# A ConvNeXt-V2 block on one core: convolution in two stretches, larger gelu tiles, statistics in halves

## The chip, the cores and the metric

The kernel runs on one core of one Trainium2 chip. The metric is device time in microseconds (us), the median of several runs; less is better. The engines are TensorE (PE in the profile, PEld for its weight loads), VectorE (DVE), ScalarE (ACT), GpSimd (POOL) and SyncE (SP, which here only issues DMAs).

## The reference

```python
# x: 1 x 512 x 512 x 96, dw: 3 x 3 x 96, w1: 96 x 384, w2: 384 x 96, all bf16
for i in range(3):
    for j in range(3):
        out = out + xp[:, i:i+H, j:j+W, :] * dw[i, j]      # depthwise 3 x 3, zero padding
h = _layernorm(out, axis=-1)                               # over the 96 channels
h = gelu(einsum('bhwc,ce->bhwe', h, w1))                   # tanh form
gx = sqrt((h * h).sum(axis=(1, 2), keepdims=True) + 1e-6)  # over all pixels
nx = gx / (gx.mean(axis=-1, keepdims=True) + 1e-6)
h = grn_gamma * (h * nx) + grn_beta + h
return x + einsum('bhwe,ec->bhwc', h, w2)
```

The sum of squares over all pixels stands between the two matrix products, so the kernel has a first part (convolution, layernorm, first product, gelu, sums of squares) and a second part (second product and the output), for which gelu values are kept, stored or computed again.

## The kernel before, in words

The image is cut into 128 blocks of GR = 4 rows, 2048 pixels by 96 channels each. The first part is a software pipeline of slots `s = 0, 1, 2, ...`. In one slot each engine works on different blocks: block `s` is convolved, the statistics of block `s - 2` are summed, another block is normalised on POOL, and the block that was convolved 14 slots or so earlier gets its first product and gelu. A dictionary `at[(s, kind)]` tells which block has which stage in which slot. Every engine object is wrapped in `InOrder`, so each engine's instructions stand in exactly the order in which the Python code calls them, and the profile shows line 35 (the wrapper) for nearly all of them; one goes by tiles.

The steps around the change, by engine:

- **Convolution, PE.** `conv_taps` makes 72 matmuls per block, in 9 rounds of 8. A matmul has 64 input rows (h = 0 or 1: upper or lower half of the array) and 32 output columns (j = 0 to 3), so the 8 of a round lie beside each other in the array. They add into three PSUM banks, `Y3` (banks 4 to 6), one for each third `i` of the channels. Both halves h write to the same bank, at different times: a bank that one half has just left may not be entered by the other half until the first half's matmuls have ended. Before, the rounds were grouped into three bursts `conv(0)`, `conv(1)`, `conv(2)` of 24 matmuls; in a burst half 0 works on bank `n` and half 1 on bank `n + 1`. Between bursts PE is drained (`pe.drain()`), except behind `conv(1)` in slots with a gelu stage, where other work stands between.
- **Evacuation, ACT.** `evac` copies `Y3` to the tile `y_bf` as bf16 (one ACTIVATE of 3 banks). The next block's convolution can't begin before that, since there is only one `Y3`.
- **Product and gelu, PE and ACT.** `mlp_units` gives `unit(bank, n)`: matmuls that fill `n` of a block's 12 banks of results and one gelu ACTIVATE over them into the tile `g`. It uses PSUM banks 0 to 3: before, a unit of two took banks 0 and 1 together, a unit of one bank 2 or 3 in turn.
- **Statistics, PE and DVE.** `stage_stats` sums `y_bf` and its square `ysq` (made by POOL) over channels with 12 + 12 tiny matmuls into a region S of PSUM bank 7. After each batch of 4 blocks `stage_moments` on DVE reads S (tile `mom`) and clears it.
- **Sums of squares.** `squares` are `bn_stats` on DVE over `g` (tile `bst`); for what they don't cover, `gram_next` gives 6 PE matmuls of `g` with itself (a region of bank 7).
- **Input.** `turn_x` on DVE transposes the loaded block (`xin` to `xT`).
- **The rest.** POOL squares `y_bf` (`ysq`) and normalises (`yn`); SP writes `yn` to DRAM and reads it back in the layout of the product (`ynT`).

114 blocks (0 to 113) pass through the slot with convolution and gelu that the change edits; the last 14 go through `mlp_tail`, without a convolution beside it. The order of calls in such a slot was: conv(0), units 0 (2 banks) and 2 (1), conv(1), units 3 (1) and 4 (2), gram_next, units 6 (1) and 7 (1), conv(2), evacuation, gram_next, units 8 (2), 10 (1), 11 (1), with the statistics between the last two.

Of the kernel before, what the change touches and what calls it, by code (L numbers as in the profile page):

```python
# [12 lines left out]
GR = 4  # L13
# [6 lines left out]
WHOLE = (0, 3, 7)  # L20
NTAIL = 14
GRB = 3


class InOrder:
# [31 lines left out]
def kernel(  # L57
# [20 lines left out]
    NI = C // 32  # L78
# [103 lines left out]
    PS = pspool.tile([128, 8, W], f32, name="PS")  # L182
    p2 = ExitStack()
    SL = PXP + 2
    with ExitStack() as p1:
# [214 lines left out]
        n = 0  # L400
# [55 lines left out]
        ybf, ysq, yns, rbcs, msts, rns, rts = ({} for _ in range(7))  # L456
# [5 lines left out]
        def conv_taps(b, spare):  # L462
            if spare:
                Ua, Ub = banks(2), banks(1)
                Y = [Ua[:, 0, :], Ua[:, 1, :], Ub[:, 0, :]]
            else:
                Y = [Y3[:, i, :] for i in range(NI)]
            mms = []
            for n in range(3):
                mms.append([(h, j, (n + h) % NI, dx) for dx in (0, -1, 1) for j in range(GR) for h in range(2)])  # L470
            flat = [m for ms in mms for m in ms]
            first = {}
            last = {}
            for n, (h, j, i, dx) in enumerate(flat):
                first.setdefault((i, j), n)
                last[i, j] = n

            def burst(n, fence=True):
                k = sum(len(ms) for ms in mms[:n])
                for h, j, i, dx in mms[n]:  # L480
                    src = b + shift(h, j)
                    o0, o1 = max(0, -dx), W - max(0, dx)
                    pe.matmul(
                        Y[i][32 * j:32 * j + 32, o0:o1],
                        lhsT=Wq[64 * h:64 * h + 64, i, dx + 1, j, :],
                        rhs=x_rows(src, 64 * h, 64 * h + 64, i, MB * (1 + dx) + o0, o1 - o0)
                        if 0 <= src < NBLK else zrow[64 * h:64 * h + 64, o0:o1],
                        start=first[i, j] == k,
                        stop=last[i, j] == k,
                    )  # L490
                    k += 1
                if n < 2 and fence:
                    pe.drain()

            def evac():
                y = ypool.tile([128, NI, W], bf16, name="y_bf")
                if spare:
                    act.activation(out=y[:, 0:2, :], in_=Ua, func=ACTF.Identity)
                    act.activation(out=y[:, 2, :], in_=Ub[:, 0, :], func=ACTF.Identity)
                else:  # L500
                    act.activation(out=y[:], in_=Y3, func=ACTF.Identity)
                ybf[b] = y

            return [lambda fence=True, n=n: burst(n, fence) for n in range(3)], evac

        def stage_sq(b, on_act):
            q = ysqpool.tile([128, NI, W], bf16, name="ysq")
# [3 lines left out]
                pool.tensor_tensor(out=q[:], in0=ybf[b][:], in1=ybf[b][:], op=ALU.mult)  # L511
            ysq[b] = q

        def stage_stats(b):
            k = batch_of[b]
            b0, n = BATCHES[k]
            for src, h in ((ybf[b], 0), (ysq.pop(b), 1)):
                for g in range(NG):
                    c0 = (b - b0) * NG + g
                    for i in range(NI):  # L520
                        pe.matmul(S[:, h, c0:c0 + (GR - 1) * n * NG + 1:n * NG],
                                  lhsT=src[:, i, g * 128:(g + 1) * 128], rhs=rowsel[:],
                                  start=False, stop=(i == NI - 1), skip_group_check=True)
# [174 lines left out]
        def mlp_units(b):  # L698
            gs[b] = gpool.tile([128, NQ, NCH, QW], bf16, name="g")[:]
            g, yt = gs[b], ynts[b]  # L700
            px0 = QC * (cm_quads(b) - 2)
            tail = flat(b)[:, 2 * QC:]

            def cm_mm(dst, j, t):
                pe.matmul(quad_out(dst), lhsT=w1p[:, j * 128:(j + 1) * 128], rhs=quad(yt[:], t), start=True, stop=True)

            def unit(bank, n):
                U = banks(n)
                if bank < 2 * NCH:
                    j, t0 = divmod(bank, 2)  # L710
                    for t in range(t0, t0 + n):
                        cm_mm(U[:, t - t0, :], j, t)
                    act.activation(out=g[:, t0:t0 + n, j, :], in_=U, func=ACTF.Gelu_apprx_tanh)
                    return
                Uf = U.rearrange("p k w -> p (k w)")
                c = c0 = (bank - 2 * NCH) * QW
                end = c0 + n * QW
                while c < end:
                    if c < px0:
                        t, j = divmod(c // QW, NCH)  # L720
                        sz = QW
                        cm_mm(Uf[:, c - c0:c - c0 + sz], j, 2 + t)
                    else:
                        k, e0 = divmod(c - px0, E)
                        sz = min(E - e0, 512 - c % 512, end - c)
                        t, r = divmod(k, GR)
                        col = (cm_quads(b) + t) * 128
                        pe.matmul(Uf[:, c - c0:c - c0 + sz], lhsT=yt[:, r, col:col + 128], rhs=w1p[:, e0:e0 + sz],
                                  start=True, stop=True)
                    c += sz  # L730
                act.activation(out=tail[:, c0:end], in_=Uf, func=ACTF.Gelu_apprx_tanh)

            def squares(j):
# [57 lines left out]
        at = {}  # L791
# [39 lines left out]
        for s in range(last_slot + 1):  # L831
# [30 lines left out]
            if mlp and mlp[0] >= TAIL0:  # L862
                assert not taps
                square_owed()
                mlp_tail(mlp[0], get)
            elif not mlp:
                if s + 3 < NBLK:
                    turn_x(s + 3)
                for f in taps:
                    f()  # L870
                if not spare:
                    spread_out()
                if evac:
                    evac()
                for b in get("sqa"):
                    stage_sq(b, True)
                for b in get("stats"):
                    stage_stats(b)
                for k in get("moments"):
                    stage_moments(k)  # L880
                if spare:
                    spread_out()
                for k in get("chain"):
                    stage_moments(k)
                    stage_chain(k)
                for k in get("turn"):
                    stage_turn(k)
                gram_next(2)
                square_owed()
            else:  # L890
                b = mlp[0]
                unit, squares, squares_rest = mlp_units(b)
                conv = lambda n, fence=True: taps[n](fence) if taps else None

                conv(0)
                unit(0, 2)
                unit(2, 1)
                squares(0)
                conv(1, False)
                spread_out()  # L900
                if s + 3 < NBLK:
                    turn_x(s + 3)
                unit(3, 1)
                unit(4, 2)
                squares(1)
                gram_next(1 if taps else 2)
                unit(6, 1)
                squares(2)
                unit(7, 1)
                for k in get("turn"):  # L910
                    stage_turn(k)
                conv(2)
                if evac:
                    evac()
                gram_next(1 if taps else 2)
                unit(8, 2)
                unit(10, 1)
                for b2 in get("stats"):
                    stage_stats(b2)
                unit(11, 1)  # L920
                for k in get("moments"):
                    stage_moments(k)
                squares_rest(2)
                square_owed()
                if is_whole(b):
                    owed.append(lambda f=squares_rest: f(3))
                grams.extend((b, c) for c in range(cm_quads(b) * QC, NQ * QC, 2 * E))
                if is_whole(b):
                    stores.extend((b, h) for h in range(3))
# [127 lines left out]
```

## Time and profile before

| | |
|---|---|
| median of 3 runs | 1480.13 us (1479.71 to 1490.58) |
| the profiled execution, first to last instruction | 1483.2 us |
| granted TensorE clock, mean | 0.994 |
| PE, DVE, ACT, POOL busy | 94%, 79%, 95%, 88% of the span |
| slots with convolution and gelu | about 101 to 885 us |
| second part (output) | about 1000 us to the end |

The profile has one execution of the program. A row of the timeline gives the start (us from the span's start), the time covered, the engine, the operation with the tiles that it writes and reads, the shapes and the number of instructions merged into the row. A row that covers several instructions ends with the last of them. On ACT and PE an instruction's row begins before its predecessor has ended, since they are pipelined; so what an instruction costs in a stream is the distance from its start to the next one's, not its own length.

### The profile page before, as it was taken

The page shows a single profiled execution, that of the slowest core. Times are in us where ns is not written, and L with a number is a line of the kernel's source. Part 1 is how long each engine was busy: PE and PEld are TensorE (multiplying, and loading weights), DVE is VectorE, ACT ScalarE, POOL GpSimd, SP SyncE. Part 2 cuts the span into 40 slices and gives each one's busy share as a digit, 9 for nine tenths or more (in the row PEclk, how much of TensorE's full clock was granted, in tenths as well). Part 3 has the DMA queues.
Part 4 walks back from the last instruction along what each step waited for, and adds up shares of the span by engine and source line. Part 5 has one row for each costly group of instructions (what it writes and reads, how often), then busy time and mean ns, then how long its engine had stood idle before and what let it go on. Part 6 is the DMA issues. An engine that isn't in the chain of part 4 may idle for free.

```text
span 1483.2 us, 54230 instructions
## 1 busy us (share of the span) xinstructions
PE 1392.2 (94%) x23125; PEld 812.3 (55%) x23125; DVE 1166.9 (79%) x2139; ACT 1415.9 (95%) x1595; POOL 1300.7 (88%) x922
## 2 busy tenths in 40 slices
PE   8889999999999999999999997789999999999998
PEld 3334444444444444444444445467777777676766
DVE  7749989999999999999999987955555555555555
ACT  6889999999999999999999999989999999998997
POOL 3459889998999999999999996559999999999997
PEclk9999999999999999999999999999999999999999
DMA  6577788887878888888888867569999999999997
GB/s 178 166 215 235 231 245 282 250 267 243 276 240 274 258 266 259 276 248 280 265 248 264 260 217 210 188 248 404 366 352 410 415 414 413 415 408 410 401 406 279
DMA packets 167768, 433.08 MB, mean 292 GB/s; under 512 B 31558, under 2 KB 81318, under 8 KB 163046
## 3 DMA queue, kind: packets, MB, share of 16 engines
q1 hardware_dynamic: 151284, 326.04, 66.8%
q0 software_dynamic: 14880, 103.43, 17.6%
q8 instruction: 181, 2.97, 0.9%
q14 instruction: 61, 0.50, 0.1%
q10 hardware_dynamic: 1362, 0.15, 0.1%
HBM read 273.30 MB, written 156.22 MB: 290 GB/s over the span
## 4 chain that ended last, share of the span: by engine, by line
PE 31%; ACT 25%; DMA 20%; DVE 10%; POOL 8%; issue 4%; SPq 3%; ACTq 0%; POOLq 0%; DVEq 0%
PE PS L35 31%; ACT g L35 18%; DMA out_dram<-o_sb 9%; ACT y_bf L35 6%; DVE bst L35 5%; POOL yn L35 4%; DMA ynT<-yn_dram 4%; SPq L35 3%; DMA rbc<-r_dram 2%; DMA xin<-in_x_dram 2%; DVE xT L35 2%; DMA yn_dram<-yn 2%; POOL ysq L35 1%; DVE o_sb L35 1%; DMA g_dram<-g 1%
## 5 line engine op out<-in xcount | busy, mean ns | idle before, releaser
L35 ACT ACTIVATE g<-PS 128x512 bf16<-128x512 f32 (+2 forms) x1062 | 727.2, 862 | 9.3 <-PE PS L35 9.1
L35 DVE BATCH_NORM_STATS2 bst<-g 128x6 f32<-128x512 bf16 x1110 | 671.3, 673 | 29.3 <-ACT g L35 28.8
L35 PE MATMUL PS<-ynT,w1p 128*128 128x512 bf16 x2181 | 610.0, 381 | 24.2 <-ACT g L35 5.4
L35 ACT ACTIVATE gr<-PS 128x1536 bf16<-128x1536 f32 x360 | 498.9, 1455 | 27.2 <-PE PS L35 18.7
L35 DVE TENSOR_TENSOR o_sb<-PS,xb 128x384 bf16<-128x384 f32 x512 | 278.0, 557 | 231.2 <-PE PS L35 184.9
L35 POOL TENSOR_TENSOR yn<-y_bf,rbc 128x1536 bf16<-128x1536 bf16 x126 | 391.6, 3111 | 75.1 <-DMA rbc<-r_dram 23.5
L325 POOL TENSOR_TENSOR xb<-xr,B2c 128x1536 f32<-128x1536 bf16 x118 | 368.4, 3133 | 7.9 <-DVE o_sb L35 5.5
L35 PE MATMUL PS<-xT,Wq 64*32 64x511 bf16 (+1 forms) x9198 | 339.7, 388 | 27.5 <-ACT y_bf L35 7.7
L35 POOL TENSOR_TENSOR ysq<-y_bf 128x1536 bf16<-128x1536 bf16 x114 | 314.0, 2755 | 14.4 <-ACT y_bf L35 14.3
L35 PEld LDWEIGHTS <-w1p 128*128 128x128 bf16 x2181 | 171.4, 98 | 221.3 <-issue 130.4
L35 PEld LDWEIGHTS <-gr 128*128 128x128 bf16 x4296 | 213.1, 98 | 75.8 <-issue 19.7
L35 PE MATMUL PS<-W2s,gr 128*128 128x96 bf16 x4224 | 224.5, 206 | 13.8 <-DVE o_sb L35 13.4
L35 PEld LDWEIGHTS <-Wq 64*32 64x32 bf16 x9216 | 112.5, 90 | 192.9 <-issue 145.9
L35 ACT ACTIVATE y_bf<-PS 128x1536 bf16<-128x1536 f32 (+2 forms) x135 | 199.4, 1483 | 17.9 <-PE PS L35 13.3
L35 DVE STREAM_TRANSPOSE xT<-xin 128x576 f32<-128x576 f32 (+1 forms) x256 | 181.8, 750 | 13.1 <-DMA xin<-in_x_dram 11.0
L35 PEld LDWEIGHTS <-g 128*128 128x128 bf16 x1704 | 105.1, 98 | 89.1 <-issue 57.4
L35 PE MATMUL PS<-w1p,ynT 128*128 128x256 bf16 (+2 forms) x822 | 125.6, 273 | 7.7 <-ACT xT L35 3.2
L35 PE MATMUL PS<-g 128*128 128x128 bf16 x1464 | 122.9, 220 | 5.0 <-DVE PS L35 4.9
L35 PEld LDWEIGHTS <-gl 128*128 128x128 bf16 x1680 | 82.9, 98 | 24.4 <-issue 2.4
L35 PE MATMUL PS<-W2s,gl 128*128 128x96 bf16 x1680 | 89.6, 206 | 1.1 <-DVE o_sb L35 0.8
L35 PEld LDWEIGHTS <-ynT 128*128 128x128 bf16 x822 | 64.1, 98 | 31.1 <-issue 13.3
L280 POOL DMA_DIRECT2D xr<-in_x_dram x115 | 63.8, 555 | 14.2 <-POOL xb L325 14.2
(106 smaller groups left out, 559.9 us busy)
## 6 DMA issues: line engine op xcount, KB each, us to landing
xin<-in_x_dram SPq DMA_DIRECT2D x126, 432.0 KB
g_dram<-g SPq DMA_DIRECT2D x105, 512.0 KB
gl<-g_dram POOLq DMA_DIRECT2D x35, 1536.0 KB, 10.9
yn_dram<-yn SPq DMA_DIRECT2D x512, 96.0 KB
ynT<-yn_dram SPq DMA_DIRECT2D x128, 384.0 KB
out_dram<-o_sb SPq DMA_DIRECT2D x127, 384.0 KB
xr<-in_x_dram POOLq DMA_DIRECT2D x123, 384.0 KB, 6.9
ynT<-yn_dram SPq DMA_DIRECT2D x85, 512.0 KB
```

The costliest lines, as they stand in the source:

```text
L35: r = f(*a, **k)
L280: pq.dma_start(out=xr[:], in_=x[0, r0:r0 + GR].rearrange("r w c -> (r w) c").rearrange("(p g) c -> p g c", g=PXP))
L325: pq.tensor_tensor(out=xb[:], in0=grp[q]["xr"][:], in1=bias[:, None, :].to_broadcast([128, PXP, C]), op=ALU.add)
```

## The change

- `conv_taps` makes the same 72 matmuls in the order that `ROUNDS` gives: in round n half h works on bank `ROUNDS[h][n]`. They are issued in two stretches, of 40 and 32 matmuls (`SPLIT`). There is no drain in or between them in slots with a gelu stage; where one half enters a bank that the other half has left in the same stretch, PE's next weight load waits for the single last matmul that the other half made there. That is once in each stretch: ahead of the fourth round of the first, on a matmul of its second, and ahead of the fourth round of the second, on a matmul of its first. In slots without a gelu stage a drain stands between the two stretches.
- The units of a block have 2, 2, 1, 1, 2, 2, 2 banks instead of 2, 1, 1, 2, 1, 1, 2, 1, 1, and alternate between banks 0, 1 and banks 2, 3: 7 gelu instructions a block instead of 9.
- The slot's order is new: units 0 and 2, conv(0), units 4, 5, 6, gram_next, unit 8, gram_next, unit 10, conv(1), evacuation. The evacuation, which had units 8, 10 and 11 behind it in the slot, is now last.
- The statistics of a block are taken in two halves: `y_bf` between units 0 and 2 (at the slot's start), `ysq` behind conv(1) (at its end).

DVE, POOL and SP keep all their instructions in the same order; ACT has 228 instructions fewer, PE 128 drains fewer.

```diff
+SPLIT = 40
+ROUNDS = ((0, 0, 0, 1, 1, 1, 2, 2, 2), (1, 1, 2, 2, 2, 0, 0, 0, 1))
...
-            mms = []
-            for n in range(3):
-                mms.append([(h, j, (n + h) % NI, dx) for dx in (0, -1, 1) for j in range(GR) for h in range(2)])
-            flat = [m for ms in mms for m in ms]
+            flat = []
+            for n in range(len(ROUNDS[0])):
+                now = [(ROUNDS[h][n], (0, -1, 1)[ROUNDS[h][:n].count(ROUNDS[h][n])]) for h in range(2)]
+                flat += [(h, j) + now[h] for j in range(GR) for h in range(2)]
+            cuts = [0, SPLIT, len(flat)]
...
+            enters, mms = {}, {}
+            for n in range(2):
+                left = {}
+                for k in range(cuts[n], cuts[n + 1]):
+                    h, j, i, dx = flat[k]
+                    if j == 0 and (i, 1 - h) in left:
+                        enters[k] = left.pop((i, 1 - h))
+                    if j == GR - 1:
+                        left[i, h] = k
...
+                    if k in enters:
+                        hold = pe.nop()
+                        tc.add_manual_dep(hold.ins, mms[enters[k]].ins.name, ...)
...
-                if n < 2 and fence:
-                    pe.drain()
...
-        def stage_stats(b):
+        def stage_stats(b, *hs):
...
-            for src, h in ((ybf[b], 0), (ysq.pop(b), 1)):
+            for h in hs or (0, 1):
+                src = ysq.pop(b) if h else ybf[b]
...
-            def unit(bank, n):
-                U = banks(n)
+            def unit(bank, n, at):
+                U = PS[:, at:at + n, :]
...
-                for f in taps:
+                for n, f in enumerate(taps):
+                    if n:
+                        pe.drain()
                     f()
...
-                conv(0)
-                unit(0, 2)
-                unit(2, 1)
-                squares(0)
-                conv(1, False)
+                unit(0, 2, 0)
+                for b2 in get("stats"):
+                    stage_stats(b2, 0)
+                unit(2, 2, 2)
+                squares(0)
+                conv(0)
                 spread_out()
                 if s + 3 < NBLK:
                     turn_x(s + 3)
-                unit(3, 1)
-                unit(4, 2)
+                unit(4, 1, 0)
+                unit(5, 1, 1)
                 squares(1)
-                gram_next(1 if taps else 2)
-                unit(6, 1)
+                unit(6, 2, 2)
                 squares(2)
-                unit(7, 1)
+                gram_next(1)
                 for k in get("turn"):
                     stage_turn(k)
-                conv(2)
+                unit(8, 2, 0)
+                gram_next(1)
+                unit(10, 2, 2)
+                conv(1)
+                for b2 in get("stats"):
+                    stage_stats(b2, 1)
                 if evac:
                     evac()
-                gram_next(1 if taps else 2)
-                unit(8, 2)
-                unit(10, 1)
-                for b2 in get("stats"):
-                    stage_stats(b2)
-                unit(11, 1)
                 for k in get("moments"):
                     stage_moments(k)
```

More of the change, by code (lines that the diff above doesn't have):

```diff
@@ L476, in conv_taps, with burst @@
                 last[i, j] = n
-            def burst(n, fence=True):
-                k = sum(len(ms) for ms in mms[:n])
-                for h, j, i, dx in mms[n]:
+            enters, mms = {}, {}
[7 more added lines that the diff above has]
+                        left[i, h] = k
+            def burst(n):
+                for k in range(cuts[n], cuts[n + 1]):
+                    h, j, i, dx = flat[k]
+                    if k in enters:
+                        hold = pe.nop()
+                        tc.add_manual_dep(hold.ins, mms[enters[k]].ins.name,
+                                          mybir.DependencyInfo(mybir.DependencyClass.Sync, mybir.DependencyReason.DATA),
+                                          reason="row tiles of one bank")
                     src = b + shift(h, j)
                     o0, o1 = max(0, -dx), W - max(0, dx)
-                    pe.matmul(
+                    mm = pe.matmul(
                         Y[i][32 * j:32 * j + 32, o0:o1],
@@ L490, in burst @@
                     )
-                    k += 1
-                if n < 2 and fence:
-                    pe.drain()
+                    mms[k] = mm
             def evac():
@@ L502, in evac @@
                 ybf[b] = y
-            return [lambda fence=True, n=n: burst(n, fence) for n in range(3)], evac
+            return [lambda n=n: burst(n) for n in range(2)], evac
         def stage_sq(b, on_act):
@@ L892 @@
                 unit, squares, squares_rest = mlp_units(b)
-                conv = lambda n, fence=True: taps[n](fence) if taps else None
+                conv = lambda n: taps[n]() if taps else None
+                unit(0, 2, 0)
[3 more added lines that the diff above has]
+                squares(0)
                 conv(0)
-                unit(0, 2)
-                unit(2, 1)
-                squares(0)
-                conv(1, False)
                 spread_out()
```

## The prediction

> **What bounds the kernel now.** I read the page's busy line, then the busy times of the stretch in which every slot does the same work (250 to 850 us, 85 slots; columns: PE, PEld, DVE, ACT, POOL, granted clock, DMA share, GB/s), then its waits.
>
> ```profile
> PE 1392.2 (94%) x23125; PEld 812.3 (55%) x23125; DVE 1166.9 (79%) x2139; ACT 1415.9 (95%) x1595; POOL 1300.7 (88%) x922
> ...
> 250.00:850.00 600.00, 576.34 (x10453) 283.62 (x10456) 581.64 (x1028) 598.54 (x850) 565.43 (x422) 1.00 0.85 262
> ...
> ACT g L35 <- PE PS L35: 1.3, 3, 0.7
> PE PS L35 <- ACT y_bf L35: 1.7, 11, 0.2
> ```
>
> ACT is covered for 598.5 of 600 us, which is 7.04 us a slot; DVE 581.6/85 = 6.84, POOL 6.65. So no engine but ACT could be taken down far: below 6.84 us a slot DVE stops it, that is 0.2 us or 3% of this stage. But "covered" is not "working", because an ACT row begins while its predecessor still runs. The starts of one slot on ACT show that:
>
> ```profile
> 610.47 1.58 ACT L35 ACTIVATE y_bf<-PS 128x1536 bf16<-128x1536 f32 x1
> 611.80 1.16 ACT L35 ACTIVATE g<-PS 128x1024 bf16<-128x1024 f32 x1
> 612.70 0.75 ACT L35 ACTIVATE g<-PS 128x512 bf16<-128x512 f32 x1
> 613.18 0.76 ACT L35 ACTIVATE g<-PS 128x512 bf16<-128x512 f32 x1
> 613.78 1.08 ACT L35 ACTIVATE g<-PS 128x1024 bf16<-128x1024 f32 x1
> ...
> 617.51 1.56 ACT L35 ACTIVATE y_bf<-PS 128x1536 bf16<-128x1536 f32 x1
> ```
>
> From start to start: the evacuation takes 1.33 us, a gelu of two banks 0.90, of one bank 0.48. One slot is 1.33 + 3 x 0.90 + 6 x 0.48 = 6.91 us, yet the period is 617.51 - 610.47 = 7.04. The missing 0.12 lies before 613.78 (613.18 + 0.48 = 613.66). PE's rows say why:
>
> ```profile
> 610.97 0.44 PE L35 MATMUL PS<-rowsel,y_bf 128*128 128x4 bf16 x12
> 611.28 0.44 PE L35 MATMUL PS<-rowsel,ysq 128*128 128x4 bf16 x12
> ...
> 612.10 0.43 PE L35 MATMUL PS<-xT,Wq 64*32 64x512 bf16 x8
> 612.55 0.42 PE L35 MATMUL PS<-xT,Wq 64*32 64x511 bf16 x8
> 613.09 0.82 PE L35 MATMUL PS<-ynT,w1p 128*128 128x512 bf16 x3
> 613.31 0.38 PE L35 MATMUL PS<-ynT,w1p 128*128 128x512 bf16 x1
> 613.84 0.88 PE L35 MATMUL PS<-xT,Wq 64*32 64x512 bf16 x24
> 614.65 0.85 PE L35 MATMUL PS<-ynT,w1p 128*128 128x512 bf16 x3
> 614.91 0.38 PE L35 MATMUL PS<-ynT,w1p 128*128 128x512 bf16 x1
> ```
>
> So a closed loop sets the slot. Evacuation start to first convolution matmul (Y3 is free): 612.10 - 610.47 = 1.63. conv(0) with its drain: 613.09 - 612.10 = 0.99. The second matmul of unit(0, 2): +0.22. From a matmul's start to the gelu that reads it: 613.78 - 613.31 = 0.47. Then gelus up to the next evacuation, 0.90 + 0.48 + 0.48 + 0.90 + 0.48 + 0.48 = 3.72. Sum 7.03: the loop explains the period, and the three gelus behind the evacuation (0.90 + 2 x 0.48 = 1.86) fail to cover the way evacuation - conv(0) - gelu by 0.12.
>
> **The change, part by part.** DVE, POOL and SP keep their instructions in the same order; what moves is on PE and ACT.
>
> *Gelus.* 9 become 7 a slot, 228 fewer in 114 blocks. Two pairs merge: 2 x (2 x 0.48 - 0.90) = 0.12 us. ACT's own work falls to 5 x 0.90 + 2 x 0.48 + 1.33 = 6.79.
>
> *Drains.* Three rounds of eight matmuls without a drain behind them take 614.65 - 613.84 = 0.81, with one 0.99, so a drain costs 0.18 and one goes per slot. A round more costs (612.55 - 612.10)/2 = 0.225.
>
> *Waits on single matmuls.* In conv(0) the weight load ahead of round 4 waits for the end of round 2's last matmul. That matmul starts about 0.27 into the stretch and lasts 0.38, so ends at 0.65; what follows a finished wait begins 0.11 later on PE (the drained burst ends at 612.98, its successor starts at 613.09): 0.76, where round 4 would by itself start at 0.675. Cost 0.08. Bounds: 0, or a drain's 0.18. In conv(1) the watched round lies three rounds back, so the wait is over at about 0.54 of 0.675: cost 0, upper bound again 0.18. Queued behind such a wait are the rest of the stretch and all later matmuls.
>
> *The new order*, followed around the loop. Evacuation to conv(0): 1.63 as before, as the two units and the y_bf statistics ahead of it on PE need (from the end of conv(1)) 0.31 + 0.43 + 0.31 + 0.43 + 0.09 and end about 0.2 us before Y3 is free. conv(0) of five rounds: 0.81 + 2 x 0.225 + 0.08 = 1.34. First matmul of unit(4, 1) to its gelu: 0.47. That is 3.44 after the evacuation began, where ACT has only 1.33 + 0.90 + 0.90 = 3.13 of work: ACT waits 0.31, more than today's 0.12. Then gelus 4 and 5: 0.96. Now the gelu of unit(6, 2). From its start to the next evacuation ACT has 3 x 0.90 = 2.70; but unit(10, 2) needs its banks: release 614.91 - 613.78 = 1.13, two matmuls and the switch to small tiles 0.22 + 0.31 = 0.53, four rounds of conv(1) to the end of the last matmul 0.675 + 0.425 = 1.10, and 0.09 to ACT: 2.85, a second wait of 0.15. Loop: 1.63 + 1.34 + 0.47 + 0.96 + 2.85 = 7.25 against 7.03, +0.22 us a slot. What hid the last third of the convolution before was gelu 8, 10 and 11 behind the evacuation; now nothing stands there but the next slot's first two gelus, which conv(0) already uses up.
>
> *Statistics in halves.* The cost is in the order, once per batch of four blocks. The y_bf half for the next batch now comes right behind unit(0), 0.43 us after the ysq half of the batch before, and must find the sums cleared:
>
> ```profile
> 615.05 0.26 DVE L35 TENSOR_SCALAR mom<-PS 128x128 f32<-128x128 f32 x1
> 615.41 0.17 DVE L35 MEMSET PS<- 128x128 f32 x1
> ...
> 615.63 0.27 PE L35 MATMUL PS<-g 128*128 128x128 bf16 x2
> ```
>
> Read-out to next PE row: 0.58. With 0.17 for the last statistics matmul (twelve start over 0.27 us and end after 0.44) and 0.09 to the next engine (0.47 less a matmul's 0.38), that half starts 0.84 after the last ysq matmul instead of 0.45; minus the 0.2 of slack, conv(0) is 0.18 late, 0.05 a slot. Queued behind it are unit(2, 2) and conv(0), so ACT feels it whole. Lower bound 0; upper: DVE comes to the read-out 1 us late, 0.25 a slot. Its row today stands 3.5 us behind the statistics (611.6 against 615.05), but it has 4 x 6.84 = 27.4 us of work for 29 us, so I take it as in time.
>
> *Moved at no cost.* gram_next, turn_x and stage_turn stay beside PE's or DVE's waits (PE waits about 0.4 us for gelu 5's bank anyway). unit(0) needs its ynT 2.4 us earlier after the evacuation; POOL, with 6.65 us of work in 7.25, gains that lead within a few batches. If it did not, the slot would be POOL's and DMA's, no longer than today's 7.03. Ramp slots lose one drain of two, which nobody waits for. From 885 us on nothing changes.
>
> **Sum.** From 101.2 to 879.1 us there are 110 such slots: +110 x 0.27 = +29.7. They now take 777.9 where 110 x 7.03 is 773.3; the 4.6 us come from a few late slots (POOL waiting for a DMA), which a longer slot covers: -4.6. Net +25. The profiled execution's own span is 1483.2, 3.1 above the median of the runs, 1480.1; I carry the difference over: 1480 + 25 = 1505.
>
> **Rivals.** (1) *ACT's saving counts, faster.* If conv(0) were no obstacle, ACT's 6.79 and DVE's 6.84 would set the slot: -0.19 x 110 = -21, 1459. The ACT group without idle time speaks for it; against it, 3.44 us of chain over 3.13 us of work: it needs five rounds and a wait in 1.03 us, where three rounds alone take 0.81. Chance 0.07. The Trainium skill, ScalarE: Activation LUTs, section "What ACT_TABLE_LOAD costs", gives an ACTIVATE a fixed 186 ns of which about 93 overlap back to back; merging two would then save 93 ns each and 228 of them 21 us. The rows here show 0.06 each, and neither counts while ACT waits for PE.
>
> (2) *No change.* The waits cost nothing, rounds run at 0.215, the memset is early, conv(1) is ready in time: 1.63 + 1.22 + 0.47 + 0.96 + 2.75 = 7.03 to 7.10, less the 4.6: 1476 to 1490. Chance 0.18.
>
> (3) *DVE at the memset sets the slot.* The read-out waits for the ysq half behind conv(1), PE's next half waits for the memset; if DVE arrives 1 us late in each batch (after its own waits for POOL's rstd or an input), 0.25 a slot comes on top, 0.25 x 110 = 27: 1505 + 27, some 1530. For it speaks that its row stands 3.5 us late today; against it, the 1.6 us a batch that it has to spare. It decides once DVE's batch with its waits is over 29 us. Chance 0.15.
>
> **How the numbers follow.** My forecast has 0.60. Its own range is 1490 (waits and memset free: +0.13 x 110 - 4.6) to 1518 (a drain's price in conv(0), a little in conv(1)). Reaching to the rivals: 1482 to 1530. Over 1% (15 us, about what a measurement here tells from no change) slower: forecast nearly whole, rival 3 and the edge of 2, 0.75; within 1%: 0.17; faster: 0.08.
>
> **What would show it.** After: y_bf evacuations 7.2 to 7.3 apart; ACT starts 3.4 us after an evacuation with the third gelu (not 3.13), and the evacuation some 0.15 after ACT was ready; conv(0) rows x40 of 1.3 us; PE waiting for DVE's memset once in four slots. Wrong if the evacuations are under 7.0 apart (then conv(0) took under 1.05 us), or if ACT's third gelu follows the second after 0.90.

## The result: 0.4% slower, and the profile after

| | before | changed |
|---|---|---|
| median of 20 runs each | 1482.01 us (1474.31 to 1490.58) | 1488.51 us (1480.92 to 1495.01) |
| ratio to before, 95% interval | 1 | 1.0037 [1.0023, 1.0051] |
| span of the profiled execution | 1483.2 | 1489.5 |
| first evacuation with a gelu stage, start | 101.2 | 102.6 |
| from there through 110 slots | 777.9 | 788.4 |
| last of these evacuations to the second part's scaled weights (`W2s`) | 91.4 | 88.2 |
| `W2s` to the end | 512.7 | 510.3 |

The change costs 6.5 us, the interval allows 3 to 8 (a repeat below gives less). The forecast was 25 us more: the sign was right, the size was four times too large. Below, every ratio is to the kernel before on the same chip; its median there lies between 1482 and 1490.

In the changed kernel the wrapper is line 37. Its page's line of busy times, and the busy times of its engines from 250 to 850 us (columns as in the prediction):

```profile
PE 1395.9 (94%) x23125; PEld 824.5 (55%) x23125; DVE 1171.9 (79%) x2139; ACT 1418.1 (95%) x1367; POOL 1299.8 (87%) x922
```

```profile
250.00:850.00 600.00, 572.12 (x10324) 288.39 (x10324) 580.38 (x1019) 594.63 (x672) 562.16 (x422) 1.00 0.84 260
```

84 slots fit in where 85 did: 672/8 ACT instructions, 7.14 us each. Its waits in the same stretch (total us, times, longest us):

```profile
PEld L37 <- PE PS L37: 32.0, 84, 0.4
PE PS L37 <- ACT g L37: 17.2, 84, 0.2
...
PE PS L37 <- DVE PS L37: 5.3, 21, 0.5
ACT g L37 <- PE PS L37: 5.1, 21, 0.5
```

Each slot has one wait of PE's weight load for PE (the watched matmul of conv(0)). PE waits for DVE, and ACT for PE, 21 times each: once per batch of four slots. A shorter stall of ACT does not show in this view, since a row that begins 0.1 late still begins before its predecessor's end. One slot on ACT, and then PE's part in it, from the timeline of the changed kernel:

```profile
605.14 1.45 ACT L37 ACTIVATE y_bf<-PS 128x1536 bf16<-128x1536 f32 x1
606.49 1.02 ACT L37 ACTIVATE g<-PS 128x1024 bf16<-128x1024 f32 x1
...
608.40 0.60 ACT L37 ACTIVATE g<-PS 128x512 bf16<-128x512 f32 x1
...
609.37 1.03 ACT L37 ACTIVATE g<-PS 128x1024 bf16<-128x1024 f32 x1
...
612.25 1.45 ACT L37 ACTIVATE y_bf<-PS 128x1536 bf16<-128x1536 f32 x1
```

```profile
606.64 1.40 PE L37 MATMUL PS<-xT,Wq 64*32 64x512 bf16 x40
607.98 0.39 PE L37 MATMUL PS<-ynT,w1p 128*128 128x512 bf16 x1
...
610.46 0.60 PE L37 MATMUL PS<-w1p,ynT 128*128 128x256 bf16 x4 [0.20 <-ACT g L37]
610.98 1.11 PE L37 MATMUL PS<-xT,Wq 64*32 64x511 bf16 x32
```

The prediction's loop can be walked on these rows: evacuation to conv(0) 606.64 - 605.14 = 1.50 (1.63 was forecast), conv(0) 607.98 - 606.64 = 1.34 (1.34), matmul to its gelu 608.40 - 607.98 = 0.42 (0.47), gelus 4 and 5 0.97 (0.96), gelu 6 to the next evacuation 612.25 - 609.37 = 2.88 (2.85). The sum is 7.11 here, and 7.085 at the median of all such slots, not 7.25. Three terms held; the two that join ACT's rows to PE's came out too long.

### The profile page after: what moved, and what is told of

Read it like the earlier page. It is cut to its first block, busy times and chain, and to the rows that moved or that the text cites. A ratio compares the mean times of both kernels' runs of the same rounds, so it can differ in the third digit from the quotient of the medians.

```text
span 1489.5 us, 53874 instructions
## 1 busy us (share of the span) xinstructions
PE 1395.9 (94%) x23125; PEld 824.5 (55%) x23125; DVE 1171.9 (79%) x2139; ACT 1418.1 (95%) x1367; POOL 1299.8 (87%) x922
## 4 chain that ended last, share of the span: by engine, by line
PE 31%; ACT 29%; DVE 16%; DMA 11%; issue 6%; POOL 5%; SPq 2%; ACTq 0%; DVEq 0%; POOLq 0%
PE PS L37 31%; ACT g L37 24%; DVE bst L37 10%; DMA out_dram<-o_sb 6%; DVE xT L37 3%; ACT y_bf L37 3%; POOL yn L37 2%; SPq L37 2%; POOL xb L327 2%; DMA ynT<-yn_dram 2%; DMA rbc<-r_dram 1%; DMA yn_dram<-yn 1%; ACT xT L37 1%; DVE o_sb L37 1%; DVE mom L37 1%
## 5 line engine op out<-in xcount | busy, mean ns | idle before, releaser
L37 ACT ACTIVATE g<-PS 128x1024 bf16<-128x1024 f32 (+1 forms) x834 | 705.2, 940 | 15.1 <-PE PS L37 14.8
L37 PE MATMUL PS<-ynT,w1p 128*128 128x512 bf16 x2181 | 619.8, 381 | 21.1 <-ACT g L37 12.1
L37 PE MATMUL PS<-xT,Wq 64*32 64x511 bf16 (+1 forms) x9198 | 321.5, 389 | 14.0 <-ACT y_bf L37 3.0
L37 PEld LDWEIGHTS <-w1p 128*128 128x128 bf16 x2181 | 168.0, 97 | 152.8 <-issue 90.0
L37 ACT ACTIVATE y_bf<-PS 128x1536 bf16<-128x1536 f32 (+2 forms) x135 | 186.0, 1383 | 16.5 <-PE PS L37 12.0
L37 PEld LDWEIGHTS <-g 128*128 128x128 bf16 x1704 | 110.3, 97 | 44.0 <-issue 9.2
L37 PEld LDWEIGHTS <-ynT 128*128 128x128 bf16 x822 | 73.7, 97 | 69.8 <-issue 54.4
L37 PEld LDWEIGHTS <-y_bf 128*128 128x128 bf16 x1536 | 55.3, 96 | 46.2 <-issue 21.3
```

The lines of the kernel that those rows point to most:

```text
L37: r = f(*a, **k)
```

## The experiments

### The loop's prices: two repeats and an ACT stream without partners

The changed kernel and the kernel before were each run once more, unedited, to see how much of a span belongs to one execution.

> The changed kernel once more, beside the kernel before on the same chip as the next two: 0.3 to 0.5% slower, 7.07 us slots with one of 7.3 in four.

> The kernel before once more, for a second profile of it: median slot 7.03 to 7.04 us (ACT's own 7.03), few late slots (two over 7.5 us in the first profile).

Measured: 1.0016 [0.9992, 1.0041] and 0.9997 [0.9975, 1.0020]. For the changed kernel that is less than the 0.3 to 0.5% expected, and its interval holds "no change" as well; what the change costs in all is known no better than these two figures, 1.0037 and 1.0016. The slots repeat: 89 slots in the middle of the stage took 636.1 us in both executions of the changed kernel, 628.7 and 629.0 in those of the kernel before. The first 100 us and the second part don't (`W2s` to end 510.3 and 513.9 changed, 512.7 and 508.5 before), so the -2.4 us in the table's last line is no effect of the change. Where less than 5 us matter, compare the 89 slots and not the spans.

What do ACT's instructions cost, if nothing makes ACT wait? One kernel leaves out the whole computation: ACT alone works through full PSUM banks, 100 gelus of one bank, 100 of two, 100 evacuations, then 20 slots in the order of before and 20 in the order of the changed kernel.

```diff
+    for n in (1, 2):
+        for k in range(100): gelu(n)
+    for k in range(100): evac()
+    for k in range(20):
+        for n in (2, 1, 1, 2, 1, 1, 0, 2, 1, 1): gelu(n) if n else evac()
+    for k in range(20):
+        for n in (2, 2, 1, 1, 2, 2, 2, 0): gelu(n) if n else evac()
```

> ACT by itself: only ACTIVATEs out of PSUM that was filled once, with no other engine in the way (it leaves out the whole computation; the output is a copy of x). 100 gelus of one bank, 100 of two, 100 evacuations of three, then 20 slots in the order of before and 20 in that of the change. Theory D (in a queue an ACTIVATE's row starts earlier and earlier, so a few start-to-start distances read too short; the end-to-end distances are the cost): 0.49, 0.917 and 1.343 us each, 7.03 a slot before and 6.90 after. Theory S (start-to-start is the cost, as the prediction took it): 0.478, 0.904, 1.331, slots of 6.91 and 6.79.

Its timeline: the 200 gelus as one row, the hundred evacuations as one, then two evacuations one slot of before apart, and two one slot of the changed order apart:

```profile
5.17 140.77 ACT L84 ACTIVATE g<-PS 128x512 bf16<-128x512 f32 x200 [3.15 <-DVE PS L76]
143.35 136.92 ACT L88 ACTIVATE y_bf<-PS 128x1536 bf16<-128x1536 f32 x100
...
307.93 5.61 ACT L88 ACTIVATE y_bf<-PS 128x1536 bf16<-128x1536 f32 x1
...
314.96 5.61 ACT L88 ACTIVATE y_bf<-PS 128x1536 bf16<-128x1536 f32 x1
...
428.93 5.82 ACT L88 ACTIVATE y_bf<-PS 128x1536 bf16<-128x1536 f32 x1
...
435.74 5.92 ACT L88 ACTIVATE y_bf<-PS 128x1536 bf16<-128x1536 f32 x1
```

An evacuation alone does not cover 5.6 us: in the changed kernel, behind a wait, its row covers 1.45. When ACT has a queue of ready work, each row starts a little earlier than its predecessor's end would have it and so grows longer than the last. In the changed order, which had not yet come to its steady lead, starts lie 435.74 - 428.93 = 6.81 apart, but ends 441.66 - 434.75 = 6.91. Only ends tell the cost. The hundred evacuations end at 143.35 + 136.92 = 280.27, the gelus ahead of them at 5.17 + 140.77 = 145.94: 1.343 us each. In the same way 0.490 us for a gelu of one bank and 0.917 for two (100 of each: 140.7). Before's slot is then 6 x 0.490 + 3 x 0.917 + 1.343 = 7.03, and the changed one's 2 x 0.490 + 5 x 0.917 + 1.343 = 6.91; the rows above show both (314.96 - 307.93 at equal length; 6.91 by ends).

This undoes the prediction's first finding, and the rule given with the profile before, that an instruction's cost in a stream is the distance from its start to the next one's. The prediction took ACT's work of the kernel before as 6.91 by starts and saw 0.12 us of waiting in the 7.04. By ends there is no wait: in the rows shown in the prediction the gelu that "waited" ends at 613.78 + 1.08 = 614.86, which is 0.92 after its predecessor's end at 613.94, just what a gelu of two banks costs. In the ordinary slots of the kernel before, ACT alone was the bound.

### Was there a loop over PE in the kernel before?

If so, taking the drain out of its conv(0) must shorten the slot; if ACT's work is the slot, nothing happens.

```diff
-                conv(0)
+                conv(0, False)
+                    if n == 1 and k == 24:
+                        hold = pe.nop()
+                        tc.add_manual_dep(hold.ins, made[23].ins.name, ...)
```

> The kernel before, with the drain behind conv(0) taken out; instead conv(1), which comes three other matmuls later, waits ahead of its first weight load for conv(0)'s last matmul, long ended. Theory A: conv(0) 0.99 to 0.81 us, ACT's stall of 0.12 ahead of the first gelu goes, slot 7.03 to 6.91, 13 us less than before: near 1469. Rival C (POOL with its DMAs, or DVE, holds the slot near 7.0 whatever ACT does): 0 to 5 us less, 1477 to 1482, and ACT idle or PE waiting for ysq, ynT or xT instead.

Measured: 1489.28 us, 0.9998 [0.9975, 1.0022]. The evacuations of the timeline stay where ACT's work puts them, as these rows of ACT and then of PE show:

```profile
515.61 1.65 ACT L35 ACTIVATE y_bf<-PS 128x1536 bf16<-128x1536 f32 x1
...
522.64 1.65 ACT L35 ACTIVATE y_bf<-PS 128x1536 bf16<-128x1536 f32 x1
```

```profile
517.31 0.88 PE L35 MATMUL PS<-xT,Wq 64*32 64x512 bf16 x24
518.23 0.87 PE L35 MATMUL PS<-ynT,w1p 128*128 128x512 bf16 x3
```

7.03 apart, the figure of the ACT stream. Where nothing holds up the next unit, conv(0) takes 0.81 without its drain; but in most slots the first matmul of unit(0, 2) follows 0.92 after conv(0)'s first (518.23 - 517.31), where it was 0.99, because PE now waits there for ACT's gelu of unit 8, which holds the same two banks. The drains that the change takes out were off the path: 0.18 us each, worth nothing.

### The loop of the changed kernel: moving the cut, moving the wait

With 6.907 of work per slot, everything above it is a stall. By ends, the changed kernel has two: 0.085 ahead of gelu 4 (conv(0) is late) and 0.101 ahead of the evacuation (conv(1) is late); 6.907 + 0.085 + 0.101 = 7.09, measured 7.085. The cut `SPLIT` moves rounds of eight matmuls between the two places.

```diff
-SPLIT = 40
+SPLIT = 48   # the second experiment: 32
```

> The changed kernel with stretches of 48 and 24 matmuls. Theory A (chain evacuation, conv(0), gelu 4 and chain gelu 6, conv(1), evacuation in series): ACT's stall ahead of gelu 4 grows from 0.10 to 0.32 us, that ahead of the evacuation goes from 0.14 to 0, +0.08 a slot, about 8 us more than the changed kernel, near 1497; the evacuation's row is then long again (1.5 us or more) and conv(0) starts 1.6 us after it. Rival B (only the sum of both stretches or another engine sets the slot): 1488, no change.

> The changed kernel with stretches of 32 and 40 matmuls. Theory D (chain by row ends: conv(0) 0.23 shorter takes away ACT's stall of 0.10 ahead of gelu 4 and no more, conv(1) 0.22 longer adds all of it to the stall ahead of the evacuation): slot 7.07 to 7.18, 10 us over the changed kernel. Rival B (the sum of both stretches sets the slot): no change.

Cut 48: 1498.37 us, 1.0062 [1.0035, 1.0089], slot 7.206. Cut 32: 1508.82 us, 1.0118 [1.0086, 1.0149], slot 7.305, where 7.18 was expected. Rows of the timeline: ACT with cut 48, PE with cut 48, PE with cut 32:

```profile
603.05 1.49 ACT L37 ACTIVATE y_bf<-PS 128x1536 bf16<-128x1536 f32 x1
604.38 2.00 ACT L37 ACTIVATE g<-PS 128x1024 bf16<-128x1024 f32 x2
606.57 3.83 ACT L37 ACTIVATE g<-PS 128x512 bf16<-128x512 f32 x5 [0.19 <-PE PS L37]
610.25 1.49 ACT L37 ACTIVATE y_bf<-PS 128x1536 bf16<-128x1536 f32 x1
```

```profile
604.59 1.61 PE L37 MATMUL PS<-xT,Wq 64*32 64x512 bf16 x48 [0.21 <-ACT y_bf L37]
...
609.14 0.88 PE L37 MATMUL PS<-xT,Wq 64*32 64x512 bf16 x24
```

```profile
607.63 1.40 PE L37 MATMUL PS<-xT,Wq 64*32 64x511 bf16 x40
...
610.69 1.15 PE L37 MATMUL PS<-xT,Wq 64*32 64x512 bf16 x32
```

With cut 48 a gap stands on ACT in every slot ahead of gelu 4, and none ahead of the evacuation: stalls of 0.306 and 0, 6.907 + 0.306 = 7.21. With cut 32 it is the reverse, 0 and 0.394: 7.30. Most of the miss of 0.12 has a plain reason. With this cut the second stretch has not one but two entries into a bank left in the same stretch, and one of them watches a matmul of only two rounds earlier, as the wait of conv(0) does; conv(1) grew by 0.30 where 0.22 was expected, a round of 0.23 and 0.055 of waiting. Most of the rest lies in the figures that the expectation started from (a slot of 7.07 and a stall of 0.10 for 7.085 and 0.085). The two stalls add, because one slot runs through both: this is the loop of the prediction, confirmed in kind.

What does the wait on a single matmul cost, if the matmul is not yet done? Here each of the two waits watches the last matmul issued.

```diff
-                        tc.add_manual_dep(hold.ins, mms[enters[k]].ins.name, ...)
+                        tc.add_manual_dep(hold.ins, mms[k - 1].ins.name, ...)
```

> The changed kernel, each of its two waits put on the last matmul of the round just ahead (which has only been issued) instead of one two or three rounds back. Theory D (both stretches lie in series in the slot's chain and a wait costs what a drain does, 0.18 us, when its matmul is still running): conv(0) 1.33 to 1.43, conv(1) 0.18 longer, slot 7.07 to 7.3, 25 to 30 us more than the changed kernel. Rival (the stretches are hidden behind ACT, or the waits cost little wherever they stand): within 5 us of it.

Measured: 1552.25 us, 1.0428 [1.0399, 1.0457], slot 7.705. PE's rows:

```profile
602.98 1.61 PE L37 MATMUL PS<-xT,Wq 64*32 64x512 bf16 x40
...
607.53 1.52 PE L37 MATMUL PS<-xT,Wq 64*32 64x511 bf16 x32
```

conv(0) went from 1.32 to 1.53, conv(1) from 1.03 to 1.45: +0.21 and +0.42, together 0.63, and the slot rose by 7.705 - 7.085 = 0.62. That is the loop once more, to the hundredth: what either stretch loses, the slot loses. The expectation had a rise of 0.23, from 7.07 to 7.3, too little for a wait on a matmul that has only just been issued, twice. In conv(0) that is the last matmul of the third round; in conv(1), where the wait stands ahead of the fourth round's second matmul, it is the first of the same round. Inside the changed kernel itself the wait of conv(0) moves its fourth round from 0.228 to 0.283 after the third, so it costs 0.055; that of conv(1) costs nothing. Both had been forecast (0.08 and 0).

### Evacuating earlier

Would it help to put conv(1) and the evacuation behind unit 6, so that two gelus stand behind the evacuation again? (In this run the statistics are whole again, and conv(1) first waits for the last matmul of conv(0).)

```diff
                 unit(6, 2, 2)
                 squares(2)
+                conv(1)
+                if evac:
+                    evac()
                 gram_next(1)
...
                 unit(10, 2, 2)
-                conv(1)
...
-                if evac:
-                    evac()
```

> The changed kernel with conv(1) and the evacuation moved up behind unit(6), ahead of units 8 and 10, and the statistics whole at the slot's end; a wait for conv(0)'s last matmul stands ahead of conv(1). Theory A: four gelus now stand between evacuation and gelu 4, no stall is left on ACT, its 6.79 us and DVE's 6.84 set the slot: 6.85 to 6.9, that is 15 to 20 us under the kernel before, 1462 to 1467. Rival C (POOL and its DMAs hold the slot near 7.0): 1477 to 1482, with PE waiting for ysq or ynT.

Measured: 1522.67 us, 1.0222 [1.0187, 1.0258], slot 7.50. The expectation overlooked a wait; the view of waits, 250 to 850 us, shows it:

```profile
ACT g L37 <- PE PS L37: 39.2, 80, 0.5
```

0.5 us in every slot. Unit 2 of the next slot needs the banks of gelu 10, which is now directly ahead of it on ACT, and conv(0) is queued behind unit 2 on PE. From the start of gelu 10 to gelu 4 PE needs 1.08 (banks free) + 0.43 + 0.09 (unit 2) + 1.33 (conv(0)) + 0.43 = 3.36 us, ACT in that time has gelus 10, 0 and 2, 3 x 0.917 = 2.75: a stall of 0.61, and 6.907 + 0.61 = 7.52. With two pairs of banks, what stands ahead of a unit on ACT is part of conv(0)'s way.

### The statistics whole again

```diff
                 unit(0, 2, 0)
-                for b2 in get("stats"):
-                    stage_stats(b2, 0)
...
                 for b2 in get("stats"):
-                    stage_stats(b2, 1)
+                    stage_stats(b2)
```

> The changed kernel with the statistics taken whole again, y_bf and ysq together behind conv(1). Theory A (the slot is a chain through ACT and PE, and once per batch the y_bf half waits for DVE's memset): the long slot of each batch (7.34 us between evacuations, against 7.07) goes, 0.27 x 27 batches, so about 7 us less than the changed kernel, near 1481. Rival B (the memset costs nothing, the long slot has another cause): stays at 1488 and keeps a 7.3 us slot in every four.

Measured: 1485.53 us, 0.9979 [0.9954, 1.0005], slot 7.077. Rows of PE, then of DVE, in a batch's first slot of the changed kernel, and after them the edited kernel's only wait of PE for DVE in the same 600 us:

```profile
590.52 0.46 PE L37 MATMUL PS<-rowsel,ysq 128*128 128x4 bf16 x12
590.83 0.59 PE L37 MATMUL PS<-ynT,w1p 128*128 128x512 bf16 x2
591.62 0.44 PE L37 MATMUL PS<-rowsel,y_bf 128*128 128x4 bf16 x12 [0.20 <-DVE PS L37]
```

```profile
591.01 0.29 DVE L37 TENSOR_SCALAR mom<-PS 128x128 f32<-128x128 f32 x1
591.40 0.17 DVE L37 MEMSET PS<- 128x128 f32 x1
```

```profile
PE PS L37 <- DVE PS L37: 0.6, 1, 0.6
```

The y_bf half waits for the memset, as forecast, and that slot takes 7.33 instead of 7.07: 0.26 a batch, 0.065 a slot (forecast 0.18 and 0.05). Without the split the 21 waits become one. DVE comes to the read-out in time (591.01, 0.03 after the ysq row's end) in 18 of the 22 batches of the 89 slots, and 0.3 us late in four, whose slots take about 7.6; so the third rival, a DVE 1 us late in each batch, is out. 110 x 0.065 makes 7 us for the halves. The ratios fit that: 1.0037 and 0.9979 lie 0.0058 or 9 us apart, the repeat's 1.0016 and 0.9979 some 5 us. But the traced execution of the edited kernel does not show the gain: its 89 slots took 636.6 us, as many as the changed kernel's 636.1, since eight of them came late, up to 9.77 us. Its POOL waits 13.2 us for `rbc` from 250 to 850 us, where that of the changed kernel waits 4.8; what `rbc` is comes next.

### Where does the rest go? Merging gelus alone, and a shorter chain on POOL

One pair merged in the kernel before takes ACT's work to 6.97 without any loop:

```diff
-                unit(6, 1)
+                unit(6, 2)           # with PS[:, 2:4, :]
                 squares(2)
-                unit(7, 1)
```

> The kernel before with units 6 and 7 made into one of two banks, nothing else: 8 gelus a block. Theory D (ACT's work alone sets the slot before: 7.03 us with no stall): one merge takes 0.06 off, slot 6.97, 7 us less than before. Rival C (POOL with its DMAs holds the slot near 7.0): no change, slots 7.0 to 7.05 and more late slots.

Measured: 1488.14 us, 0.9999 [0.9976, 1.0021]. The median slot is 7.01, nearer to 6.97 as it should be, but the mean is 7.15: 12 of the 89 slots in the middle take over 7.5 us, where the kernel before has two, in its repeat three. What the shorter slot wins is lost to late ones. Who is late? In the kernel before without its drain, too, eight of them were late, and the waits of that kernel from 250 to 850 us name the partners:

```profile
PEld L35 <- DMA ynT<-yn_dram: 11.7, 12, 3.0
DVE xT L35 <- DMA xin<-in_x_dram: 11.3, 7, 3.4
POOL yn L35 <- DMA rbc<-r_dram: 9.4, 11, 1.5
```

In the merged kernel POOL's wait for rbc is 16.0 us, 15 times. PE waits for ynT, which comes by DMA from POOL's yn, which waits for rbc, the broadcast rstd that POOL's own batch chain makes (variance, two Newton steps, write, read back). If this chain is the second bound, shortening it must help every version, and the changed one least, since its longer slots give the chain time. So three kernels leave out the second Newton step, part of the computation: 4 POOL instructions fewer per batch, 35.6 us less of POOL's busy time.

```diff
-NEWTON_ITERS = 2
+NEWTON_ITERS = 1
```

> The kernel with units 6 and 7 merged (e7), and with one Newton step for the reciprocal root on POOL instead of two (it leaves out the second, four instructions or 1.5 us of POOL a batch, so its values are coarser). Theory C (POOL's chain with its DMAs is next behind ACT and ate e7's gain in late slots): the late slots go back to a handful and the slot to 6.97, 7 us less than before. Rival (the late slots come from the DMAs alone): as e7, no faster than before.

> The kernel before with one Newton step instead of two (the second is left out). Theory D and C: ACT's 7.03 holds the slot, so no more than the few late slots can be won, 0 to 4 us. If POOL itself set the slot before: 1.5 us in each of 27 batches, up to 40 us less.

> The changed kernel with one Newton step instead of two on POOL (the second is left out), to be set beside e11, the kernel before with the same. Theory E (the change costs its slots 0.10 us each, about 11 us; the kernel before loses half of that again in ramp, late slots and tail, where POOL's chain is late, and the slower slot of the change spares it this): with POOL relieved in both, the difference grows from 3 to 6 us to about 10 or 11, so near 0.994 or 0.995 of the kernel before where e11 had 0.9875. Rival (the change's cost in the slots is not whole in the end for another reason, as a faster second part): the difference stays at 3 to 6 us, 0.990 to 0.991.

| | gelus | two Newton steps | one | its slots, mean |
|---|---|---|---|---|
| before | 2,1,1,2,1,1,2,1,1 | 1 | 0.9875 [0.9843, 0.9907] | 7.034 |
| before, one pair merged | 2,1,1,2,2,2,1,1 | 0.9999 [0.9976, 1.0021] | 0.9847 [0.9816, 0.9877] | 6.985 |
| changed | 2,2,1,1,2,2,2 | 1.0037 [1.0023, 1.0051] | 0.9965 [0.9948, 0.9981] | 7.145 |

The busy times of the kernel before, then of the changed one, both with one step, 250 to 850 us:

```profile
250.00:850.00 600.00, 578.50 (x10485) 285.07 (x10486) 587.82 (x1035) 600.00 (x855) 548.37 (x348) 1.00 0.87 265
```

```profile
250.00:850.00 600.00, 572.15 (x10332) 288.42 (x10331) 580.66 (x1020) 594.78 (x672) 537.52 (x337) 1.00 0.86 262
```

With the shorter chain ACT of the kernel before is covered for all of the 600 us, its slot is ACT's 7.03, and no slot is late. The changed kernel keeps its 7.145: its loop, not POOL, sets it. So with one step the change costs 0.9965/0.9875 = 1.009, some 13 us (by the two intervals 8 to 19), which agrees with 110 x (7.15 - 7.03) = 13.2; with both steps it costs half of this, by the medians.

The gain of the kernel before, 18 us, was far from the 0 to 4 expected. Its traced executions show 5 to 9 us of it in the 110 slots (772.7 against 777.9 and 781.3) and 4 to 8 at the first part's end (87.2 against 91.4 and 94.8, to `W2s`); the rest is not located. Of the half that both steps hide, the traces show 2.5 us in the 89 slots: the changed kernel's take 7.4 us more than the other's with both steps, and 9.9 with one. The first part's end, too, is shorter in the changed kernel, by 3.2 us, in the repeats 7.2. The waits there, 870 to 1000 us, first of the kernel before, then of the changed one:

```profile
POOL yn L35 <- DMA rbc<-r_dram: 11.2, 2, 6.4
...
DVE rt L35 <- POOL rstd L35: 7.8, 2, 4.7
...
PEld L35 <- DMA ynT<-yn_dram: 2.8, 5, 1.2
```

```profile
POOL yn L37 <- DMA yn_dram<-yn: 8.7, 1, 8.7
...
POOL yn L37 <- DMA rbc<-r_dram: 4.6, 1, 4.6
...
DVE rt L37 <- POOL rstd L37: 2.1, 1, 2.1
...
PEld L37 <- DMA ynT<-yn_dram: 0.4, 1, 0.4
```

The waits along the chain (rstd, rbc, ynT) fall from 21.8 to 7.1 us. Where POOL of the changed kernel waits long, it is for one of its own buffers to be written out, that is, POOL is ahead. Whether the chain makes this difference is not shown: with one step in both kernels the end still differs by 2.9 us (87.2 and 84.3), while POOL waits longer for `rbc` in the changed one (12.1 us against 5.3).

Can the chain be relieved with the whole computation kept? The first four of its instructions, which make the first guess `ri`, were given to DVE, in the merged kernel and in the changed one with whole statistics.

```diff
-                stage_rstd(k, pool)
+                stage_rstd(k, dve)
```

> The kernel with units 6 and 7 merged (e7), and the four small instructions of stage_rstd on DVE instead of POOL; nothing is left out. Theory E: POOL has 1.6 us less a batch, DVE some 0.7 more (27.4 to 28.1 us of 4 x 6.97 = 27.9): late slots go in part, slot 6.97 to 7.03, tail and ramp shorter: 5 to 15 us less than before. Rival (DVE now sets the batch): slots of 7.05 and more, no gain.

> The changed kernel with whole statistics (e1) and stage_rstd on DVE; nothing is left out. Theory E: slot 7.07 as in e1, no late slots, shorter ramp and tail: 5 to 10 us less than e1, 0.990 to 0.995 of the kernel before. Rival (DVE): no gain on e1.

Measured: 1485.85 us, 1.0001 [0.9984, 1.0019], and 1504.11 us, 1.0120 [1.0099, 1.0142]. Both expectations were missed: the first kernel gained nothing, the second lost 1.4% against the same kernel with the chain on POOL. The same work is only waited for elsewhere, as the waits show, first of the merged kernel, then of the changed one:

```profile
POOL nt L35 <- DVE ri L35: 22.0, 21, 1.6
```

```profile
PE PS L37 <- DVE PS L37: 20.8, 19, 2.1
```

POOL, whose Newton steps begin with `nt`, now stands once a batch until DVE is through its queue, and PE until DVE comes to the memset. Of the kernels that compute everything, none was faster than the kernel before by more than the measurement's uncertainty. A different chain that saves these instructions was not tried.

## Why the prediction was right in sign and wrong in size

- **What failed: the loop's sum, 7.25 for 7.085.** The step was "from start to start: the evacuation takes 1.33 us, a gelu of two banks 0.90, of one bank 0.48", and the links taken over from it. In the kernel before ACT hardly ever idles (it is covered for 598.5 of 600 us), so its rows start before their turn: the evacuation's row covers 1.58 us there and 1.45 in the changed kernel, where ACT waits ahead of it. "Evacuation to conv(0) 1.63" counted these 0.13 into the loop; it is 1.50, and from the evacuation's end to conv(0) it is 0.05 in both kernels. "Matmul to its gelu 0.47" was read where the gelu waited for ACT, not for the matmul; it is 0.42 to 0.43. "Release 1.13" is 1.08, but the end of conv(1) to the evacuation is 0.16 and not 0.09. With these the walk gives 1.50 + 1.34 + 0.43 + 0.96 + 2.87 = 7.10. Put in ACT's terms: its own work in a slot is 6.91 and not 6.79, and its two waits are 0.085 and 0.101 and not 0.31 and 0.15. Against the measured 7.085 the sum was 0.165 us a slot too long, 110 x 0.165 = 18 us of a miss of 18.5; the smaller differences below nearly cancel.
- **A closed loop sets the slot before: wrong.** 7.04 agreed with the sum 7.03, but ACT's work alone is 7.03. The sum closed because its terms were read from the same rows as the period; that was no proof.
- **Right: PE's terms.** conv(0) 1.34 (1.32 to 1.34 measured), the wait in it 0.08 (0.055), the wait in conv(1) 0, the memset 0.05 a slot (0.065). Right in kind, too long in size: the second stall, ahead of the evacuation, 0.15 (0.10).
- **Right in kind: the credit of 4.6 us for late slots.** The 89 slots of before hold about 3 us of them (628.7 against 626.0 with the shorter chain); in the changed kernel none of the 89 is over 7.2, apart from the 22 in which PE waits for the memset. The prediction had nothing for the first part's end (-3.2 us in the table, -7.2 in the repeats), whose cause stays open.
- **The account.** Stage +10.5: 7.4 in the 89 slots, which is the 9.9 with one Newton step less 2.5 for late slots, and 3.1 in the 21 slots ahead of them (1.2 in the repeats). End of the first part -3.2, first 100 us +1.4, second part -2.4 (not repeated). Sum +6.3 in span.
- **The rivals.** ACT's saving alone (1459) is out: the slot is 7.085, not 6.84. "No change", given 0.18, has the result in its range of 1476 to 1490, but not for its reasons: its slot of 7.03 to 7.10 leads only to 1476 to 1483, conv(0) took 1.32 and not its 1.22 (its rounds took 0.23, with the wait 0.28), the evacuation was late and the memset too. Only its waits were nearly as cheap as it said. That its range held is luck: it kept the 1.63 that is 1.50, and so made up for what it left out. The ACT stream gives what a merge saves: 0.490 - 0.427 = 0.063 us, where 0.427 is what each further bank adds (0.917 - 0.490). The Trainium skill, ScalarE: Activation LUTs, section "What ACT_TABLE_LOAD costs", has 186 ns fixed for an ACTIVATE with immediate scale and bias, of which about 93 overlap, so that a merge would save an estimated 93 ns; the measurement decides. Its 0.833 ns per element, by which 512 would take an estimated 0.427 us, agrees with the stream.

## What to carry to other kernels

Where an engine has a queue of ready work and its rows overlap, read an instruction's cost from end to end, not from start to start. Before a loop over several engines is blamed for a period, add up the busiest engine's own work: if that alone makes the period, the loop does not. In a stage where one engine is full and a second one's chain is nearly as long, a small gain on the first can be eaten by the second, and a small loss partly refunded; measure it with the second one relieved. Two instructions merged on the full engine help only as long as the new order leaves it work to do while the other engine's longest stretch runs.

## What the runs showed of the hardware

- **ACT's rows run ahead.** With a queue of ready work each ACTIVATE's row began about 0.0125 us earlier relative to its predecessor's end, until an evacuation's row covered 5 to 6 us for 1.34 us of work. The lead is lost when ACT waits: in the changed kernel, behind a wait, the row covers 1.45.
- **A wait on a matmul costs by how fresh it is.** On a matmul made two rounds earlier it cost 0.055 us, on one made three rounds earlier nothing. On the one just issued it cost 0.21 us more in conv(0) and 0.42 in conv(1), more than a whole drain at 0.18.
- **POOL's small instructions counted, though POOL was not full.** Leaving out 35.6 us of them, spread over the run, brought 18 us of total time, 1.25%, on an engine that was busy for 88% of the span.
